# Retention of the first 768 tokens: two tokens to a partition, 64-row tiles, all masks ahead of v, decays about the middle of 256 tokens

## The chip, the cores and the metric

The kernel runs on one core of a Trainium2 chip. The metric is the device time of one execution in microseconds (us), 205.38 as the median of three runs before the change (205.08 to 205.7). Engines: PE is the tensor engine (PEld its weight loads), DVE the vector engine, ACT the scalar engine, POOL is GpSimd, SP issues most DMAs; "SPq" and "ACTq" are the queues of SP and ACT that issue DMAs.

## The reference

A retention layer (a linear attention whose state decays) for 4 batches, 8 heads, 768 tokens and 64 channels a head feeds a two-layer network with mish as its activation:

```python
gamma = 1.0 - 2.0 ** (-5.0 - np.arange(H))            # one decay per head
for t in range(S):
    state = gamma * state + einsum('bhd,bhe->bhde', k[:, :, t], v[:, :, t])
    y[:, :, t] = einsum('bhd,bhde->bhe', q[:, :, t], state) / sqrt(D)
x = y.transpose(0, 2, 1, 3).reshape(B * S, H * D)      # 3072 x 512
h = x @ w_in                                           # 512 x 2048
out = (h * tanh(log1p(exp(h)))) @ w_out                # 2048 x 512
```

## The kernel before

The retention is computed in chunks. A chunk is 128 tokens of one batch, all 8 heads (six chunks a batch, 24 in all, number `g`). Within a chunk: scores are k transposed times q (`at`, in PSUM, the matmuls' memory), a mask keeps what is not ahead of its token (`am`, by DVE), `present` multiplies `am` with v, `past` adds q times the state of the chunk before, `outer` is k times v, summed into the state. The decay is put on q, k or v as a power of gamma when the fp32 inputs are cast to fp16 (`casts`, L220), and a state is multiplied by gamma^128 when it is handed on (`gcm` L309, `gch` L451). The result is written, transposed, as `xt`.

The network takes tokens in blocks: block 0 has four chunks (512 tokens), every later one two. `g1` (L540) is the first matrix product with mish by ACT, `g2_mm` (L561) the second, `seven` (L626) the second product of the blocks from 2 on in a form with seven products in place of eight; it needs sums of w_out parts, `tmat` (L599 to L602), which DVE computes during block 1.

The order of instructions on each engine is the order in which the program issues them; nothing is moved by a scheduler. Each engine works its own queue in that order, and an instruction waits for the data and the buffers that it needs.

Block 0 (`first_block`, L725): SP loads the first q in two halves (four tokens to a partition, so 1024 contiguous bytes each), then k and v of chunk 0, 1, 2, 3 in turn (one token to a partition, 256 contiguous bytes for each head), then w_in in six loads, w_out in three, and q and v of chunk 4. Scores have 64 rows (channels of one head) and 128 columns, `present` 128 rows and 64 columns, and `outer`, `past` and the state's addition by an identity matmul use all 128 rows and columns, two heads at a time. `spin` (L250) issues matmuls whose result nobody reads; they fill PE's time while it waits. k is cast by ACT (L229), v by POOL (L233). Behind the retention DVE casts w_in (`cast_win`, L161, eight half slices) as it lands.

While block 0 runs through `g1` and `g2_mm`, `plan` (L769) hangs further work behind numbered steps: casts of w_out, the loads of chunks 4 and 5 (`load_more`, three of them issued by ACT), their casts, transposes by PE (`turn`), scores, state and `y_two` for block 1. From chunk 6 on, q and k are transposed by DMA (`turn_by_dma`, L237), and the retention runs in tiles of 64 rows and 64 columns, so that four matmuls with different quarters of the array can work at a time (`score`, `outer_half`, `y_mm`); a half chunk's state is `mid` (L436), a chunk's state is `suh` and `sth` (L445). A one-column copy of the result (`seen`, L522) stands between matmuls that add to the same PSUM bank from different rows. Buffers come from rotating pools; a pool's `bufs` is how many there are.

Of the kernel before, what the change touches and what calls it, by code (L numbers as in the profile page):

```python
# [16 lines left out]
def kernel(  # L17
# [12 lines left out]
    P = 128  # L30
# [16 lines left out]
    gamma = (1.0 - 2.0 ** (-5.0 - np.arange(H))).astype(np.float64)  # L47
    jj = np.arange(C)
    mid = (C - 1) / 2.0
    qs_np = np.stack([BOOST * scale * g ** (jj - mid) for g in gamma], 1).astype(np.float32)  # L50
    vs_np = np.stack([BOOST * g ** (mid - jj) for g in gamma], 1).astype(np.float32)
    spread = [qs_np[(jj * CPB + r) % C] for r in range(CPB)]
    boost_np = np.full((C, H), BOOST, np.float32)
    qvs_np = np.ascontiguousarray(np.concatenate([qs_np, vs_np, *spread, boost_np], 1))
# [5 lines left out]
    tpp = ctx.enter_context(tc.tile_pool(name="rn_tp", bufs=2))  # L60
# [14 lines left out]
    qvs = cpool.tile([P, (3 + CPB) * H], FP32, name="qvs")  # L75
    nc.scalar.dma_start(qvs, nc.inline_tensor(qvs_np, name="qvs_c").ap())
    qs, vs = qvs[:, :H], qvs[:, H:2 * H]
    qs_spread = qvs[:, 2 * H:(2 + CPB) * H].rearrange("p (r h) -> p h r", r=CPB)
    boosts = qvs[:, (2 + CPB) * H:]
    ident = cpool.tile([P, P], FP16, name="ident")  # L80
    tri = cpool.tile([P, C], FP32, name="tri")
    gcm = cpool.tile([P, HP, P], FP32, name="gcm")
    gch = cpool.tile([P, HP, D], FP32, name="gch")
    warm = cpool.tile([P, 1], FP32, name="warm")
# [4 lines left out]
    nc.gpsimd.memset(tri, 0.0)  # L89
    nc.gpsimd.affine_select(  # L90
        out=tri, in_=tri, compare_op=ALU.is_gt, fill=1.0, base=0,
        pattern=[[-1, C]], channel_multiplier=1)

    tri_half = cpool.tile([P, D], FP32, name="tri_half")

    tri_first = cpool.tile([P, CPB, C // CPB], FP32, name="tri_first")
    nc.gpsimd.memset(tri_first, 0.0)
    nc.gpsimd.affine_select(
        out=tri_first, in_=tri_first, compare_op=ALU.is_gt, fill=1.0, base=0,
        pattern=[[-1, CPB], [-CPB, C // CPB]], channel_multiplier=1)  # L100
# [4 lines left out]
    nc.vector.memset(gcm, 0.0)  # L105
    for h in range(H):
        o = 64 * (h % 2)
        nc.vector.memset(gcm[o:o + 64, h // 2, o:o + 64], float(gamma[h] ** C))

# [3 lines left out]
    qfirst_t = cpool.tile([P, HP, CPB, P], FP16, name="qfirst_t")  # L113
# [9 lines left out]
    def room(g):  # L123
        loaded[g] = [
            None if nm == "q" and g < CPB else
            lpool.tile([P, H, D], FP32, name=nm + "f", tag=nm + "f", bufs=4 if nm == "q" else 6)
            for nm in "qkv"]
# [67 lines left out]
    def turn_first_q(qf, half, on_act):  # L195
        a, n = half * (H // 2), H // 2
        q16 = castp.tile([P, CPB, n, D], FP16, name="qfirst16", bufs=1, tag=f"qfirst16_{half}")
        nc.vector.tensor_tensor(
            q16.rearrange("p r h d -> p h r d"), qf[:, a:a + n],
            qs_spread[:, a:a + n].unsqueeze(3).broadcast_to((P, n, CPB, D)), op=ALU.mult)  # L200
        t_ps = mmps.tile([P, n // 2, CPB, P], FP16, name="t_ps", tag="mm")
        for i in range(n // 2):
            for r in range(CPB):
                nc.tensor.transpose(t_ps[:, i, r], q16[:, r, 2 * i:2 * i + 2], ident)
        dst = qfirst_t[:, a // 2:(a + n) // 2]
        if on_act:
            nc.scalar.copy(dst, t_ps)
        else:
            nc.vector.tensor_copy(dst, t_ps)

    def turn_k(g):
        k16 = cast[g][1]
        t_ps = mmps.tile([P, HP, C], FP16, name="t_ps", tag="mm")
# [705 lines left out]
```

## Time and profile before

| what | us |
|---|---|
| median of three runs | 205.38 |
| profiled execution | 205.68 |
| its span | 203.9 |
| granted TensorE clock | 0.998 |
| first w_in matmul (L549) starts | 19.58 |
| first w_out matmul (L563) starts | 33.70 |
| block 1's first w_in matmul starts | 51.37 |
| block 2's first w_in matmul starts | 67.92 |

```profile
## 2 busy tenths in 40 slices
PE   7998999999999999999999998999999999999993
PEld 2554444445864788887888887888888888888882
DVE  3696554257999448459596564736854953655062
ACT  2333665043541452452363362463363453541640
POOL 3245000426995141952645616606607500000000
PEclk9999999999999999999999999999999999999999
DMA  5999999999999999699999999999990710200102
GB/s 178 238 220 342 379 387 365 224 304 205 206 230 250 220 223 217 145 204 247 170 171 279 195 195 258 184 200 256 171 195 3 159 50 3 103 3 35 71 27 77
```

Each column is one fortieth of the span, 5.1 us. A digit is the busy share of the engine in tenths. GB/s is what the DMA engines moved: about 220 in the second and third column, where k and v of block 0 are loaded, and 340 to 390 in the next four, where the weights are.

A line of the timeline has start, duration, engine, line, operation, tile written and read, shape, count, and in brackets the idle time ahead of it with what ended it.

### The profile page before, as it was taken

The page shows a single profiled execution, that of the slowest core. Times are in us where ns is not written, and L with a number is a line of the kernel's source. Part 1 is how long each engine was busy: PE and PEld are TensorE (multiplying, and loading weights), DVE is VectorE, ACT ScalarE, POOL GpSimd, SP SyncE. Part 2 cuts the span into 40 slices and gives each one's busy share as a digit, 9 for nine tenths or more (in the row PEclk, how much of TensorE's full clock was granted, in tenths as well). Part 3 has the DMA queues.
Part 4 walks back from the last instruction along what each step waited for, and adds up shares of the span by engine and source line. Part 5 has one row for each costly group of instructions (what it writes and reads, how often), then busy time and mean ns, then how long its engine had stood idle before and what let it go on. Part 6 is the DMA issues. An engine that isn't in the chain of part 4 may idle for free.

```text
span 203.9 us, 6059 instructions
## 1 busy us (share of the span) xinstructions
PE 196.7 (96%) x2629; PEld 149.7 (73%) x2629; DVE 121.4 (60%) x217; ACT 86.7 (43%) x154; POOL 72.3 (35%) x88
## 2 busy tenths in 40 slices
PE   7998999999999999999999998999999999999993
PEld 2554444445864788887888887888888888888882
DVE  3696554257999448459596564736854953655062
ACT  2333665043541452452363362463363453541640
POOL 3245000426995141952645616606607500000000
PEclk9999999999999999999999999999999999999999
DMA  5999999999999999699999999999990710200102
GB/s 178 238 220 342 379 387 365 224 304 205 206 230 250 220 223 217 145 204 247 170 171 279 195 195 258 184 200 256 171 195 3 159 50 3 103 3 35 71 27 77
DMA packets 99994, 38.69 MB, mean 190 GB/s; under 512 B 90496, under 2 KB 94080, under 8 KB 99968
## 3 DMA queue, kind: packets, MB, share of 16 engines
q1 hardware_dynamic: 96704, 37.50, 87.0%
q10 hardware_dynamic: 3264, 0.82, 2.4%
q8 instruction: 20, 0.33, 0.7%
q14 instruction: 6, 0.05, 0.1%
HBM read 27.29 MB, written 6.29 MB: 165 GB/s over the span
## 4 chain that ended last, share of the span: by engine, by line
PE 67%; DMA 12%; SPq 9%; DVE 8%; POOL 1%; issue 1%; ACT 1%; DVEq 0%; ACTq 0%
PE h_ps L549 33%; PE o_ps L646 23%; SPq L131 7%; DMA kf<-in_k_dram 6%; PE o_ps L563 4%; DMA wi<-in_moe_w_in_dram 3%; PE y_ps L482 3%; DMA qkt<-qk 2%; DVE tmat L601 1%; DVE tmat L602 1%; DVE tmat L599 1%; PE at L398 1%; SPq L239 1%; DVE tmat L600 1%; PE u_ps L405 1%
## 5 line engine op out<-in xcount | busy, mean ns | idle before, releaser
L549 PE MATMUL h_ps<-xt,win 128*128 128x256 f16 (+1 forms) x704 | 86.4, 282 | 0.7 <-DVE win L166 0.5
L549 PEld LDWEIGHTS <-win 128*128 128x128 f16 x704 | 68.4, 98 | 16.6 <-DVE win L166 1.0
L557 ACT ACTIVATE g<-h_ps 128x512 f16<-128x512 f32 x96 | 57.3, 597 | 49.2 <-PE h_ps L549 49.2
L233 POOL TENSOR_TENSOR v<-vf,qvs 128x512 f16<-128x512 f32 x24 | 27.5, 1146 | 19.0 <-DMA vf<-in_v_dram 18.8
L226 POOL TENSOR_TENSOR qk<-qf,qvs 128x512 f16<-128x512 f32 x20 | 20.9, 1046 | 30.3 <-DMA qf<-in_q_dram 24.1
L646 PEld LDWEIGHTS <-gsum 128*128 128x128 f16 x288 | 27.0, 98 | 3.9 <-DVE gsum L615 0.2
L646 PE MATMUL o_ps<-tmat,gsum 128*128 128x256 f16 x216 | 26.6, 273 | 0.0
L646 PEld LDWEIGHTS <-g 128*128 128x128 f16 x216 | 21.1, 98 | 2.4
L563 PE MATMUL o_ps<-wout,g 128*128 128x512 f16 x96 | 22.6, 380 | 0.0
L231 POOL TENSOR_TENSOR qk<-kf,qvs 128x512 f16<-128x512 f32 x18 | 21.1, 1171 | 1.5 <-DMA kf<-in_k_dram 1.3
L615 DVE TENSOR_TENSOR gsum<-g 128x512 f16<-128x512 f16 x18 | 9.1, 508 | 19.5 <-ACT g L557 19.4
L652 ACT COPY snap<-o_ps 128x256 f32<-128x256 f32 x27 | 10.0, 372 | 19.5 <-PE o_ps L646 19.5
L660 DVE TENSOR_TENSOR osb<-o_ps,snap 128x256 f32<-128x256 f32 x27 | 11.4, 424 | 10.8 <-PE o_ps L646 6.8
L646 PE MATMUL o_ps<-wout,g 128*128 128x256 f16 x144 | 17.2, 273 | 0.0
L563 PEld LDWEIGHTS <-g 128*128 128x128 f16 x96 | 8.8, 98 | 9.4
L822 POOL COPY summed<-gsum 128x1 f16<-128x1 f16 x6 | 1.1, 187 | 36.7 <-DVE gsum L620 26.4
L536 ACT CAST xt<-y_ps 128x512 f16<-128x512 f32 x13 | 7.2, 587 | 15.2 <-PE y_ps L482 15.2
L442 DVE TENSOR_TENSOR mid<-u_ps,sth 128x256 f16<-128x256 f32 x15 | 6.3, 422 | 11.4 <-PE u_ps L405 11.1
L253 PE MATMUL at<-ident 128*128 128x512 f16 (+1 forms) x34 | 10.3, 429 | 1.4 <-POOL ident L86 1.4
L471 DVE TENSOR_TENSOR am<-at,tri_half 128x1024 f16<-128x1024 f32 x9 | 10.9, 1214 | 0.0
L451 DVE TENSOR_TENSOR sth<-suh,gch 128x256 f16<-128x256 f32 x15 | 9.0, 602 | 0.6
L646 PE MATMUL o_ps<-wout,gsum 128*128 128x256 f16 x72 | 9.4, 273 | 0.0
(81 smaller groups left out, 176.5 us busy)
## 6 DMA issues: line engine op xcount, KB each, us to landing
kf<-in_k_dram SPq DMA_DIRECT2D x23, 256.0 KB, 5.1
vf<-in_v_dram SPq DMA_DIRECT2D x23, 256.0 KB, 5.3
out_dram<-osb SPq DMA_DIRECT2D x22, 256.0 KB, 3.2
qf<-in_q_dram SPq DMA_DIRECT2D x19, 256.0 KB, 5.2
wt<-in_moe_w_out_dram SPq DMA_DIRECT2D x3, 1024.0 KB, 10.1
wi<-in_moe_w_in_dram SPq DMA_DIRECT2D x4, 512.0 KB, 7.4
wi<-in_moe_w_in_dram SPq DMA_DIRECT2D x2, 1024.0 KB, 10.8
qfirst<-in_q_dram SPq DMA_DIRECT2D x2, 512.0 KB, 4.6
```

Of the source, the lines that this page charges most:

```text
L131: queue.dma_start(loaded[g][n], (q, k, v)[n][b, :, c * C:(c + 1) * C].rearrange("h p d -> p h d"))
L226: nc.gpsimd.tensor_tensor(q16, qf, qs.unsqueeze(2).broadcast_to((P, H, D)), op=ALU.mult)
L231: nc.gpsimd.tensor_tensor(k16, kf, boosts.unsqueeze(2).broadcast_to((P, H, D)), op=ALU.mult)
L233: nc.gpsimd.tensor_tensor(v16, vf, vs.unsqueeze(2).broadcast_to((P, H, D)), op=ALU.mult)
L253: nc.tensor.matmul(ats[g][:, 0, :m], ident, ident.unsqueeze(1).broadcast_to((P, m, P)), start=True, stop=True)
L471: nc.vector.tensor_tensor(am.rearrange("p a j i c -> p (a j i) c"), at.rearrange("p a j i c -> p (a j i) c"), tri_half.unsqueeze(1).broadc ...
L549: nc.tensor.matmul(h_ps[:, j], wins[s][f // 2][:, bp, f % 2 * P:(f % 2 + 1) * P], xts[blk][:, bp, :nt], start=(bp == 0), stop=(bp == NBP - 1))
L557: nc.scalar.activation(gt, h_ps, AF.Mish, scale=inv_boost3)
L563: nc.tensor.matmul(o_ps, gts[blk, fb][:, t * P:(t + 1) * P], wouts[s][:, f, cols], start=(fb == 0), stop=(fb == NFB - 1))
L646: nc.tensor.matmul(o_ps, x(f), w(f), start=first and f == 0, stop=f == n - 1, skip_group_check=True)
L652: nc.scalar.copy(x, o_ps)
L660: nc.vector.tensor_tensor(dst, o_ps, plus, op=ALU.add)
```

## The change

Three pairs of chunks (0 and 1, 2 and 3, 4 and 5: `n` = 0, 1, 2) are now handled as 256 tokens each. Partition p holds tokens 2p and 2p + 1, so that q (of pair 2), k and v are loaded in pieces of 512 contiguous bytes, each in two halves `a` of four heads, 256 KB a load. SP's order is first q, all k of pairs 0 and 1, all v of pairs 0 and 1, w_in, w_out, then q, k, v of pair 2. For pairs 0 and 1 POOL casts k with the decay and ACT casts v without it. Every retention matmul of the three pairs has 64 rows and 64 columns (`m` is the half of the partitions, 128 tokens each; `hh` the head of a pair of heads). All scores and masks of block 0 come ahead of its first use of v. The state of the middle of a pair is not multiplied; `gch` is gamma^256 and is applied once a pair, in later blocks too (`state_of`). The masks and `gch` are made by POOL, ahead of its casts of k and right behind them; `tri`, `tri_first`, `gcm`, `qfirst_t` and the functions for 128-row chunks are gone. The diff, without removed lines that the kernel above shows:

```diff
     gamma = (1.0 - 2.0 ** (-5.0 - np.arange(H))).astype(np.float64)
+    pos = np.arange(2 * C)
+    mid = (2 * C - 1) / 2.0
+    qs_np = np.stack([BOOST * scale * g ** (pos - mid) for g in gamma], 1).astype(np.float32)
+    vs_np = np.stack([BOOST * g ** (mid - pos) for g in gamma], 1).astype(np.float32)
     jj = np.arange(C)
-    mid = (C - 1) / 2.0
-    qs_np = np.stack([BOOST * scale * g ** (jj - mid) for g in gamma], 1).astype(np.float32)
-    vs_np = np.stack([BOOST * g ** (mid - jj) for g in gamma], 1).astype(np.float32)
-    spread = [qs_np[(jj * CPB + r) % C] for r in range(CPB)]
-    boost_np = np.full((C, H), BOOST, np.float32)
-    qvs_np = np.ascontiguousarray(np.concatenate([qs_np, vs_np, *spread, boost_np], 1))
+    tables = [qs_np[:C], qs_np[C:], vs_np[:C], vs_np[C:]]
+    tables += [qs_np[(jj * CPB + r) % (2 * C)] for r in range(CPB)]
+    tables += [qs_np[2 * jj + r] for r in range(2)]
+    tables += [vs_np[2 * jj + r] for r in range(2)]
+    tables += [np.full((C, H), BOOST, np.float32)]
+    qvs_np = np.ascontiguousarray(np.concatenate(tables, 1))
...
-    tpp = ctx.enter_context(tc.tile_pool(name="rn_tp", bufs=2))
+    tpp = ctx.enter_context(tc.tile_pool(name="rn_tp", bufs=4))
...
+    def keep_from(t, rows, pattern):
+        nc.gpsimd.memset(t, 0.0)
+        for n in range(2):
+            nc.gpsimd.affine_select(
+                out=t[n * D:(n + 1) * D], in_=t[n * D:(n + 1) * D], compare_op=ALU.is_gt,
+                fill=1.0, base=0, pattern=pattern, channel_multiplier=rows)
+
+    keep_from(keep_four, 2, [[1, 2], [-1, CPB], [-CPB, C // CPB]])
+    for h in range(H):
+        nc.gpsimd.memset(
+            gch[64 * (h % 2):64 * (h % 2) + 64, h // 2], float(gamma[h] ** (2 * C)))
...
+    def turn_parts(parts, dst, on_act=False):
+        t_ps = mmps.tile(list(dst.shape), FP16, name="t_ps", tag="mm")
+        turn_into(parts, dst, t_ps, on_act)
+
+    def turn_into(parts, dst, t_ps, on_act):
+        for i in range(dst.shape[1]):
+            for r in range(dst.shape[2]):
+                nc.tensor.transpose(t_ps[:, i, r], parts(i, r), ident)
...
+    def load_pair(n, nm, a, queue):
+        src = {"q": q, "k": k, "v": v}[nm]
+        queue.dma_start(
+            pairs[n][nm][a],
+            src[0, a * (H // 2):(a + 1) * (H // 2), n * 2 * C:(n + 1) * 2 * C].rearrange(
+                "h (p r) d -> p h r d", r=2))
+
+    def cast_pair(n, nm, a, scales=None, on=None):
+        src = pairs[n][nm][a]
+        if nm == "v":
+            t = castp.tile([P, 2, H // 2, D], FP16, name="v16", bufs=7)
+        else:
+            if a == 0:
+                pairs[n, nm] = castp.tile([P, 2, 2, H // 2, D], FP16, name="qk16", bufs=4)
+            t = pairs[n, nm][:, a]
+        pairs[n, nm, a] = t
+        dst = t.rearrange("p r h d -> p h r d")
+        if scales is None:
+            nc.scalar.mul(dst, src, BOOST)
+        else:
+            (on or nc.gpsimd).tensor_tensor(
+                dst, src, scales[:, a * (H // 2):(a + 1) * (H // 2)].unsqueeze(3).broadcast_to(
+                    (P, H // 2, 2, D)), op=ALU.mult)
+
+    def turn_pair(n, nm, a, on_act):
+        if a == 0:
+            pairs[n, nm + "t"] = qktp.tile([P, HP, 2, C], FP16, name="qkt", bufs=6)
+        t = pairs[n, nm, a]
+        turn_parts(lambda i, r: t[:, r, 2 * i:2 * i + 2],
+                   pairs[n, nm + "t"][:, a * (HP // 2):(a + 1) * (HP // 2)], on_act)
...
+    def pair_scores(n, a):
+        if (n, "at", a) not in pairs:
+            pair_at(n, a)
+        at, kt = pairs.pop((n, "at", a)), pairs[n, "kt"]
+        for i in range(HP // 2):
+            for r in range(2):
+                for m in range(2):
+                    for hh in range(2):
+                        b = a * (HP // 2) + i
+                        nc.tensor.matmul(
+                            as_q(at[half(m), hh, i, r], n), kt[half(hh), b, r, half(m)],
+                            pair_q(n, b, hh, m), start=True, stop=True)
+        am = tpp.tile([P, 2, HP // 2, 2, C], FP16, name="am")
+        keep = keep_four if n < 2 else keep_two
+        nc.vector.tensor_tensor(
+            am.rearrange("p h i r c -> p (h i) (r c)"),
+            at.rearrange("p h i r c -> p (h i) (r c)"),
+            keep.rearrange("p s r c -> p (s r c)").unsqueeze(1).broadcast_to((P, HP, 2 * C)),
+            op=ALU.mult)
+        pairs[n, "am", a] = am
...
+    def pair_outer(n, u, a):
+        k16, v16 = pairs[n, "k", a], pairs[n, "v", a]
+        for r in range(2):
+            for i in range(HP // 2):
+                for m in range(len(u)):
+                    for hh in range(2):
+                        nc.tensor.matmul(
+                            u[m][half(hh), a * (HP // 2) + i],
+                            k16[half(m), r, 2 * i + hh], v16[half(m), r, 2 * i + hh],
+                            start=a == 0 and r == 0 and i == 0, stop=True,
+                            skip_group_check=True)
+
+    def pair_state(n, u, m):
+        g = 2 * n + m
+        if m == 0:
+            st = stp.tile([P, HP, D], FP16, name="mid")
+            if n == 0:
+                nc.vector.tensor_copy(st, u[0])
+            else:
+                nc.vector.tensor_tensor(st, u[0], states[g - 1], op=ALU.add)
+        else:
+            su = stp.tile([P, HP, D], FP32, name="suh")
+            nc.vector.tensor_tensor(su, u[1], states[g - 1], op=ALU.add)
+            st = stp.tile([P, HP, D], FP16, name="sth")
+            nc.vector.tensor_tensor(st, su, gch, op=ALU.mult)
+        states[g] = st
+
+    def pair_present(n, y, a):
+        am, v16 = pairs[n, "am", a], pairs[n, "v", a]
+        for i in range(HP // 2):
+            for r in range(2):
+                for m in range(2):
+                    for hh in range(2):
+                        nc.tensor.matmul(
+                            y[m][half(hh), a * (HP // 2) + i], v16[half(m), r, 2 * i + hh],
+                            am[half(m), hh, i, r], start=a == 0 and i == 0 and r == 0,
+                            stop=True, skip_group_check=True)
+
+    def pair_past(n, y, m):
+        st = states[2 * n + m - 1]
         for i in range(HP):
-            nc.tensor.transpose(t_ps[:, i], k16[:, 2 * i:2 * i + 2], ident)
-        kt = qktp.tile([P, HP, C], FP16, name="kt", bufs=2)
-        nc.vector.tensor_copy(kt, t_ps)
-        qkts[g] = (qfirst_t[:, :, :, g * (C // CPB):(g + 1) * (C // CPB)], kt)
+            for hh in range(2):
+                nc.tensor.matmul(
+                    as_q(y[m][half(hh), i], n), st[half(hh), i], pair_q(n, i, hh, m),
+                    start=False, stop=True, skip_group_check=True)
...
+    def pair_xt(n, y, m, on_act=True):
+        blk = n // 2
+        if blk not in xts:
+            xts[blk] = xtp.tile([P, HP, TB], FP16, name="xt")
+        if blk == 0:
+            dst = xt_first(2 * n + m)
+        else:
+            dst = xts[blk][:, :, :2 * C].rearrange(
+                "p i (r c) -> p i r c", r=2)[:, :, :, half(m)]
+        src = y[m].rearrange("p i (r c) -> p i r c", r=dst.shape[2])
+        if on_act:
+            nc.scalar.copy(dst, src)
+        else:
+            nc.vector.tensor_copy(dst, src)
...
     def state_of(g):
         u = us.pop(g)
-        if not last_of_batch(g):
+        if last_of_batch(g):
+            return
+        st = stp.tile([P, HP, D], FP16, name="sth")
+        if g % 2 == 0:
+            nc.vector.tensor_tensor(st, u[:, 1], mids[g], op=ALU.add)
+        else:
             su = stp.tile([P, HP, D], FP32, name="suh")
             nc.vector.tensor_tensor(su, u[:, 1], mids[g], op=ALU.add)
-            st = stp.tile([P, HP, D], FP16, name="sth")
             nc.vector.tensor_tensor(st, su, gch, op=ALU.mult)
-            states[g] = st
+        states[g] = st
 
...
+        room_pair(2, "qkv")
+        for nm in "qkv":
+            for a in range(2):
+                load_pair(2, nm, a, nc.sync)
 
     def load_more():
-        load_one(CPB, 1, nc.scalar)
-        load_one(CPB + 1, 0, nc.scalar)
-        load_one(CPB + 1, 2, nc.scalar)
-        load_one(CPB + 1, 1, nc.sync)
         load_last_wout(0)
         load_last_wout(1)
-        nload[0] += 2
+        nload[0] = ncast[0] = CPB + 2
         load_to(CPB + 4)
 
     def first_block():
-        for g in range(CPB):
-            room(g)
         qf = load_first_q()
-        for g in range(CPB):
-            load_one(g, 1, nc.sync)
-            load_one(g, 2, nc.sync)
-        nload[0] = CPB
+        for n in range(2):
+            room_pair(n)
+        for nm in "kv":
+            for n in range(2):
+                for a in range(2):
+                    load_pair(n, nm, a, nc.sync)
         load_weights()
...
+        pair_at(0, 0)
+        spin(50)
         turn_first_q(qf, 0, True)
...
+        spin(14)
         turn_first_q(qf, 1, False)
...
         for n in range(2):
...
+            for a in range(2):
+                cast_pair(n, "k", a, vs_two)
+        nc.gpsimd.memset(tri_half, 0.0)
+        for n in range(2):
+            nc.gpsimd.affine_select(
+                out=tri_half[half(n)], in_=tri_half[half(n)], compare_op=ALU.is_gt, fill=1.0,
+                base=0, pattern=[[-1, D]], channel_multiplier=1)
+        keep_from(keep_two, 2, [[1, 2], [-1, 2], [-2, D]])
+        turn_pair(0, "k", 0, True)
+        spin(6)
+        pair_scores(0, 0)
+        pair_at(0, 1)
+        spin(2)
+        turn_pair(0, "k", 1, True)
+        spin(6)
+        pair_scores(0, 1)
+        pair_at(1, 0)
+        spin(2)
+        turn_pair(1, "k", 0, True)
+        spin(4)
+        cast_pair(0, "v", 0)
+        pair_scores(1, 0)
+        pair_at(1, 1)
+        spin(2)
+        turn_pair(1, "k", 1, True)
+        for n, a in ((0, 1), (1, 0), (1, 1)):
+            cast_pair(n, "v", a)
+        spin(4)
+        pair_scores(1, 1)
+        u = [mmps.tile([P, HP, D], FP32, name="u_ps", tag="mm") for _ in range(2)]
+        for a in range(2):
+            pair_outer(0, u, a)
+        for m in range(2):
+            pair_state(0, u, m)
+        y = [pool.tile([P, HP, C], FP32, name="y_ps", tag=tag)
+             for pool, tag in ((mmps, "mm"), (pxps, "px"))]
+        for a in range(2):
+            pair_present(0, y, a)
+        pair_xt(0, y, 0)
+        nc.scalar.copy(seen, y[1][:, 0, :1])
+        pair_past(0, y, 1)
+        pair_xt(0, y, 1)
+        u = banks("u_ps", D)
+        for a in range(2):
+            pair_outer(1, u, a)
+        pair_state(1, u, 0)
+        y = banks("y_ps", C)
+        for a in range(2):
+            pair_present(1, y, a)
+        for m in range(2):
+            nc.scalar.copy(seen, y[m][:, 0, :1])
+        pair_past(1, y, 0)
+        pair_past(1, y, 1)
+        pair_xt(1, y, 0, False)
+        pair_xt(1, y, 1)
         cast_win(0)
...
+        pair_state(1, u, 1)
         for s in range(1, NSL):
             cast_win(s)
+
+        def cast_qk():
+            for a in range(2):
+                cast_pair(2, "q", a, qs_two)
+            for a in range(2):
+                cast_pair(2, "k", a)
+            for a in range(2):
+                cast_pair(2, "v", a, vs_two)
+
+        def turn_two():
+            t_ps = atps.tile([P, 2, HP, 2, C], FP16, name="t_ps", tag="at")
+            for j, nm in enumerate("qk"):
+                pairs[2, nm + "t"] = qktp.tile([P, HP, 2, C], FP16, name="qkt", bufs=6)
+                turn_into(
+                    lambda i, r: pairs[2, nm, i // 2][:, r, i % 2 * 2:i % 2 * 2 + 2],
+                    pairs[2, nm + "t"], t_ps[:, j], nm == "k")
+
         plan = {
             9: [(cast_wout, 0)],
             12: [(cast_wout, 1)],
...
+            16: [(cast_wout, 2), (load_more,), (cast_qk,)],
+            23: [(cast_wout, 3, True)],
+            25: [(turn_two,)],
+            26: [(pair_scores, 2, 0)],
+            27: [(pair_scores, 2, 1)],
+            28: [(next_chunk, CPB + 2), (next_chunk, CPB + 3)],
+            29: [(outer_two,)],
+            31: [(y_two,)],
         }
...
+    def banks(name, width):
+        t = atps.tile([P, 2, TB], FP32, name=name, tag="at")
+        return [t[:, m, :HP * width].rearrange("p (i c) -> p i c", i=HP) for m in range(2)]
+
+    def outer_two():
+        u = banks("u_ps", D)[:1]
+        for a in range(2):
+            pair_outer(2, u, a)
+        pair_state(2, u, 0)
+
+    def y_two():
+        y = banks("y_ps", C)
+        for a in range(2):
+            pair_present(2, y, a)
+        for m in range(2):
+            nc.scalar.copy(seen, y[m][:, 0, :1])
+        for m in range(2):
+            pair_past(2, y, m)
+        for m in range(2):
+            pair_xt(2, y, m)
```

`banks` gives two PSUM banks of one `at` buffer. `pair_q` gives the transposed q of a pair, `as_q` views a result in the token order of q, `pair_at` takes an `at` buffer, `keep_four` and `keep_two` are the masks for q with four and with two tokens to a partition.

## The prediction

> **What bounds the kernel now.** I read the busy shares first, then the waits of TensorE, then the chain of waits, then the timeline of the first 20 us and of 50 to 68 us.
>
> ```profile
> PE 196.7 (96%) x2629; PEld 149.7 (73%) x2629; DVE 121.4 (60%) x217; ACT 86.7 (43%) x154; POOL 72.3 (35%) x88
> PE at L398 <- DMA qkt<-qk: 0.6, 1, 0.6
> PE h_ps L549 <- DVE win L166: 0.5, 1, 0.5
> PE t_ps L263 <- ACT qk L229: 0.3, 1, 0.3
> PE y_ps L482 <- DVE sth L451: 0.3, 1, 0.3
> ```
>
> PE is 96% busy, and its waits after the start are short. So a change can win only in two places: the 19.6 us before the first h_ps matmul, where much of PE's busy time is spin matmuls, and these few waits.
>
> ```profile
> 12.12 1.14 SPq L149
> 13.31 6.94 DMA wi<-in_moe_w_in_dram
> 20.27 0.69 DVE win L166
> ```
>
> In the chain of waits the first 20 us belong to SP's queue and to loads. The timeline shows the rate:
>
> ```profile
> 8.92 1.04 POOL L233 TENSOR_TENSOR v<-vf,qvs 128x512 f16<-128x512 f32 x1 [6.57 <-DMA vf<-in_v_dram]
> 11.26 1.04 POOL L233 TENSOR_TENSOR v<-vf,qvs 128x512 f16<-128x512 f32 x1 [1.29 <-DMA vf<-in_v_dram]
> 13.66 1.04 POOL L233 TENSOR_TENSOR v<-vf,qvs 128x512 f16<-128x512 f32 x1 [1.37 <-DMA vf<-in_v_dram]
> 16.01 1.04 POOL L233 TENSOR_TENSOR v<-vf,qvs 128x512 f16<-128x512 f32 x1 [1.30 <-DMA vf<-in_v_dram]
> 17.60 0.58 ACT L351 CAST xt<-y_ps 128x512 f16<-128x512 f32 x1 [1.67 <-PE y_ps L325]
> 18.77 0.75 DVE L166 CAST win<-wi 128x1024 f16<-128x1024 f32 x1 [0.54 <-DMA wi<-in_moe_w_in_dram]
> 19.58 0.61 PE L549 MATMUL h_ps<-xt,win 128*128 128x512 f16 x2 [0.45 <-DVE win L166]
> ```
>
> One chunk's k and v (512 KB) land every 2.36 us, so 1.18 us per 256 KB. The 1024-byte pieces of the first q ran at 385 GB/s (windows 3.0 to 5.0 us), the 256-byte pieces of k and v at 218 (windows 6.5 to 15). The retention ends at about 19.0 (L360) and the first w_in half is cast at 19.52: both paths end together.
>
> **The change, part by part.** The base is the profiled run: span 203.9, time 205.68, which is 0.30 above the median of the runs, 205.38. I add the differences to the median.
>
> *Loads.* A 512-byte piece is in no row. Bounds: 1.18 us per 256 KB (no gain) and 0.68 us (385 GB/s). Per piece and engine the rows give 18.4 ns at 256 bytes (1.18 us, 64 pieces) and 42.6 ns at 1024 (385 GB/s over 16 engines); on a line between them 512 bytes cost 26.5 ns, or 0.85 us. I take 0.8. The first q is usable at 6.40 as before, the first k quarter (half the heads of 256 tokens) at about 7.3, the last v at 6.40 + 8 x 0.8 + 0.2 = 13.0 instead of 16.0. The page "DMA: Bandwidth & Descriptors" of the Trainium skill (Specifications) puts line rate at 512 bytes and up; by it the quarter would be usable 0.1 us sooner and the sum 0.1 us lower.
>
> *Masks ahead of v.* Each quarter goes POOL cast, transposes, ACT copy, scores, mask. POOL: 1.04 us (L233 above), first from 7.3 to 8.35; gch and the first mask table (10 memsets and 2 selects, 0.15 to 0.4 us each by L762 and L98) are done by 4.5. Then PE transposes 0.40 (four, as L215), ACT copies 128x512: 0.59 by the line through L207 (1.01 at 1024) and L652 (0.37 at 256). First scores at 9.45, first mask at 9.9. The next transposes stand behind these scores in PE's queue, so a quarter takes copy 0.59, hand-over 0.06, scores 0.25, change back to 128 rows and spin 0.25, transposes 0.44: 1.6 us, more than POOL's 1.13 and DVE's 1.22 (L285). Fourth scores at 14.25. ACT gets there at 14.2 with three v casts to go: 0.63 each (L229), 0.54 in a row: 15.8.
>
> *Tail of the first block.* Now a relay of PE and ACT: xt 0.58 to 16.35, seen 0.2 to 16.5 (warm L104: 0.20), past 0.4, xt 0.58 to 17.55, meanwhile outer and present of the second pair to 17.65, two seen reads to 18.0, past to 18.45, xt on DVE 0.69 (L534) to 19.2, and only behind it in DVE's queue the cast of w_in, 0.69. First h_ps at 19.95, 0.37 later than now. The w_in halves (2.6 to 3 us earlier) are then all there, and the waits between 19.58 and 33.70 go: 14.12 less 64 x 0.2157 is 0.32. Net +0.05. The state's DVE steps (0.42, 0.42, 0.48 after the last mask at 15.9) lie beside ACT's relay; cover gone, they cost what they exceed it by.
>
> *Tokens 512 to 767, inside 33.7 to 51.4.* Removed: 0.43 between the q and k transposes (waiting for L229), since all six loads now go ahead of the last w_out on SP's queue and land about 8 us sooner; ACT's three issues (0.4 to 3.9 us) go too. Added: scores in 64-row form, 0.52 a block against 0.39 (42.39 to 42.78), +0.26; the k copy on ACT (1.01 against 0.69, behind one step of 0.86), +0.1; the 64-row outer between 128-row matmuls, each change of form costing (PEld idles 0.42 before 64-row blocks at 61.03 and 66.64): +0.2; y: present 0.45, past 0.45, change 0.3, wait for seen 0.35 (0 to 0.65: the four matmuls behind it stand in line), 1.55 against 1.14, +0.4. Sum: 0.26 + 0.1 + 0.2 + 0.4 - 0.43 = +0.53.
>
> *Later blocks.* An even chunk's state loses its multiply:
>
> ```profile
> 63.46 0.41 DVE L440 CAST mid<-u_ps 128x256 f16<-128x256 f32 x1
> 63.90 0.42 DVE L449 TENSOR_TENSOR suh<-u_ps,mid 128x256 f32<-128x256 f32 x1
> 64.43 0.48 DVE L451 TENSOR_TENSOR sth<-suh,gch 128x256 f16<-128x256 f32 x1
> 64.40 0.31 PE L482 MATMUL y_ps<-qkt,mid 64*64 64x64 f16 x8
> 64.97 0.31 PE L482 MATMUL y_ps<-qkt,sth 64*64 64x64 f16 x8 [0.26 <-DVE sth L451]
> 65.42 0.31 PE L482 MATMUL y_ps<-qkt,mid 64*64 64x64 f16 x8
> ```
>
> Eight such matmuls take 0.14 where nothing holds them (79.28 to 79.42), here 0.57 and 0.45: 0.74 lost to the DVE chain. That chain is late because the eight tmat subtractions take 11.5 us; beside POOL they take 1.53, alone 0.94 (59.69). With loads sooner by 2.6 to 5 us, POOL's casts of chunks 6 and 7 fall before that stretch, and 0.51 goes with L451. I take -0.9: 0.74, and 0.16 of the wait for the mask and the seen read (66.42) behind it. Bounds 0 and -1.0. What is late next is nothing there: PE's own matmuls.
>
> *The wait at 125.7* (0.62, transposed q and k). The 256-byte pieces saturate the queues again from 95 us on, but POOL's casts from 80 us on are tied to DVE's sums, thus to PE, so much of the lead is used up. Bounds 0 and -0.62; I take half, -0.3.
>
> Sum: +0.05 + 0.53 - 0.9 - 0.3 = -0.62, so 205.06 for a run like the profiled one, and 204.76, in short 204.8, against the median.
>
> **Rivals.** (1) *The relay is longer than I count.* The first gemm changes its bound from a load to some 20 hand-overs of PE, ACT and DVE; 0.07 more on each puts it at 21.35. For it: PE's queue stands at each copy and each seen, and nothing is issued past them. Against: hand-overs now take 0.05 to 0.1 (L229 ends 8.38, transposes 8.44). From a start at 20.57 on (0.62 after 19.95) it eats the whole gain; at 21.35 the sum is 1.40 - 0.62 = +0.78, so 206.2. (2) *PE's clock falls.* Without spins after the fourth scores PE works under half of the time from 14.5 to 20. In the first 5 us here the 512-column spin matmuls came every 0.43 us, and then every 0.21. If that returned for 3.8 us of h_ps, it costs 1.9: 206.7. Against: the granted clock is 1.00 in every window now, and my longest gap is 1.5 us. The page "TensorE: Matmul & The Clock Gate" of the Trainium skill (Part 1) has the clock drop after an idle window of about 3.4 us; by that it stays up. (3) *512-byte pieces land no faster*, so the change doesn't do what it says: last v at 16.1, ACT's cast to 16.75, the relay after it 1.0 later, 20.95: +1.05 for the first block; the later terms stay, -0.67 in all, less some 0.4 for the smaller lead: 205.38 + 1.05 - 0.27 = 206.2. (4) *The relay is shorter* (quarters at 1.4 instead of 1.6, and the whole 0.62 at 125.7 goes): -0.62 - 0.6 - 0.3 = -1.5, so 203.9. It speaks for it that the ACT copies may overlap (0.09 in a row now).
>
> **How the numbers follow.** Forecast 0.40, its own range 204.1 to 205.4; relay longer 0.22; clock 0.06; loads no faster 0.06; relay shorter 0.26. A measurement of this kernel can tell 0.3% (0.6 us) from no change: faster means under 204.76, slower over 206.0. The forecast lies on the first bound: 0.21 faster, 0.19 same. The longer relay is 0.18 slower and 0.04 same, the clock's fall slower, loads no faster half and half, the shorter relay 0.25 faster and 0.01 same. Faster 0.21 + 0.25 = 0.46, same 0.19 + 0.04 + 0.03 + 0.01 = 0.27, slower 0.18 + 0.06 + 0.03 = 0.27. The range reaches from beyond the shorter relay to beyond the longer one, 203.4 to 206.5; outside it lie the clock's case and the far parts of the others.
>
> **What would show it.** Right: last v cast or its landing near 13; scores about 1.6 us apart; first h_ps within 19.5 to 20.4 and no wait for win behind it; tmat near 1.0 to 1.3 us, mid, sth, mid without PE gaps. Wrong: h_ps after 20.57, granted clock under 1.00, k casts 1.18 apart on POOL, or PE waiting for ACT's seen over 0.65.

## The result, and the profile after

| what | before | after |
|---|---|---|
| median of four runs each, same chip | 205.54 (205.08 to 206.84) | 211.38 (211.28 to 212.96) |
| profiled execution | 205.68 | 211.39 |
| its span | 203.9 | 209.6 |
| granted TensorE clock | 0.998 | 0.984 |
| first w_in matmul starts | 19.58 | 23.01 |
| first w_out matmul starts | 33.70 | 38.79 |
| block 1's first w_in matmul starts | 51.37 | 58.30 |
| block 2's first w_in matmul starts | 67.92 | 74.08 |

The changed kernel is slower: the ratio is 1.029, 95% interval 1.022 to 1.036. The 5.7 us of span come stage by stage: 3.43 up to the first w_in matmul, 1.66 in block 0's first product (15.78 against 14.12), 1.84 from there to block 1's (19.51 against 17.67), then 0.77 are won in block 1 (15.78 against 16.55) and 0.46 behind it.

Lines of the page of the kernel after: busy shares, granted clock by slice, and the queue that brings instructions (packets, MB, share).

```profile
span 209.6 us, 6381 instructions
...
PE 196.3 (94%) x2794; PEld 149.8 (71%) x2794; DVE 108.2 (52%) x195; ACT 89.7 (43%) x163; POOL 72.5 (35%) x91
...
PEclk9999599999999999999999999999999999999999
...
q8 instruction: 22, 0.36, 0.7%
```

One digit of the clock differs from before: the fifth slice, 21 to 26 us, has the clock at half. PE's list of waits has new entries, among them these:

```profile
PE u_ps L300 <- issue: 2.4, 1, 2.4
...
PE t_ps L205 <- DVE qkt L209: 0.8, 1, 0.8
PE y_ps L336 <- ACT seen L877: 0.5, 1, 0.5
```

"issue" says that PE waited for nothing that the profile shows: no tile, no buffer, no DMA of the program. The timeline of the first block shows where:

```profile
16.48 0.35 PEld L300 LDWEIGHTS <-qk 64*64 64x64 f16 x26
...
16.53 0.41 PE L300 MATMUL u_ps<-v,qk 64*64 64x64 f16 x23
...
19.31 0.22 PE L300 MATMUL u_ps<-v,qk 64*64 64x64 f16 x3 [2.36 <-issue]
...
21.65 0.69 DVE L353 CAST xt<-y_ps 128x512 f16<-128x512 f32 x1 [1.66 <-PE y_ps L336]
...
22.37 0.59 ACT L351 CAST xt<-y_ps 128x512 f16<-128x512 f32 x1 [1.94 <-DVE xt L353]
...
23.01 1.45 PE L560 MATMUL h_ps<-xt,win 128*128 128x512 f16 x3 [1.47 <-ACT xt L351]
```

PE stops inside one `outer`, with three of its 32 matmuls left and all their operands there, and goes on 2.36 us later. The windows (length, busy time and count of each engine, clock, DMA share, GB/s) give the clock:

```profile
15.00:20.00 5.00, 1.81 (x111) 1.42 (x99) 2.51 (x5) 1.84 (x5) 0.00 (x0) 1.00 1.09 359
20.00:25.00 5.00, 3.05 (x21) 1.55 (x21) 3.32 (x7) 0.98 (x4) 0.00 (x0) 0.52 0.99 332
25.00:30.00 5.00, 5.00 (x20) 2.09 (x19) 3.73 (x6) 2.82 (x5) 0.00 (x0) 0.80 0.95 315
```

PE is busy for 1.81 of the 5 us from 15 to 20, and then works at half its clock from 20.19 to 27.02. The two losses of the first 39 us are these. The one of 1.84 lies in `turn_two` and `y_two`:

```profile
47.95 0.61 PE L205 MATMUL t_ps<-ident,qk 128*128 128x128 f16 x8 [0.78 <-DVE qkt L209]
49.66 0.42 PE L282 MATMUL at<-qkt 64*64 64x128 f16 x16 [0.24 <-ACT qkt L207]
...
56.51 0.41 PE L336 MATMUL y_ps<-qkt,sth 64*64 64x128 f16 x8 [0.51 <-ACT seen L877]
```

And the lines that answer to the `mid` and `sth` matmuls of before:

```profile
71.33 0.31 PE L493 MATMUL y_ps<-qkt,mid 64*64 64x64 f16 x8
71.48 0.29 PE L493 MATMUL y_ps<-qkt,sth 64*64 64x64 f16 x8
71.60 0.29 PE L493 MATMUL y_ps<-qkt,mid 64*64 64x64 f16 x8
```

They started 0.57 and 0.45 apart; now it is 0.15 and 0.12. This gain came as foreseen.

**What "issue" hides.** The queue "instruction" brings 22 packets, 0.36 MB: 16 KB each. PE's two times 2794 instructions over 22 are 254, so a packet holds about 256, or 128 pairs of a weight load and a matmul. From the start of PE's matmuls and of these packets in the trace:

```
              matmul at     PE starts    packet for the     PE starts    from packet's  idle of
kernel        the border    behind it    next border        its first    end to it      PE there
before        98            14.03        16.40 to 17.49     33.05        15.56          none
after         98            12.81        16.59 to 17.68     19.31         1.63          2.36
```

Numbers of matmuls here and in the expectations are places in PE's stream, counted in pairs; the trace's own count is 3 lower in the kernel after, so its 224th matmul ends the idle time. In the experiments the trace's 352nd and 2016th matmul end such a stop, one and fourteen times 128 later: so place 227 is the first of a piece, and the border before it is at 98, 226 less 128. In these rows the packet comes some microseconds after PE has crossed a border, and it brings what stands behind the next border. Before, PE then spends 15 us more on the piece in hand. After, 64-row tiles have twice the instructions for the same work: 16 + 32 + 32 + 8 + 29 = 117 pairs went between 14.21 and 16.94, and PE had reached matmul 226 before the packet had landed. That is theory A of the expectations below: PE ran out of instructions, and the clock fell because PE was idle.

### The profile page after: what moved, and what is told of

The parts are those of the page before. It is cut to its first block, busy times and chain, and to the rows that moved or that the text cites. A ratio compares the mean times of both kernels' runs of the same rounds, so it can differ in the third digit from the quotient of the medians.

```text
span 209.6 us, 6381 instructions
## 1 busy us (share of the span) xinstructions
PE 196.3 (94%) x2794; PEld 149.8 (71%) x2794; DVE 108.2 (52%) x195; ACT 89.7 (43%) x163; POOL 72.5 (35%) x91
## 4 chain that ended last, share of the span: by engine, by line
PE 88%; ACT 4%; DMA 3%; issue 2%; DVE 1%; POOL 1%; SPq 0%; POOLq 0%; ACTq 0%; DVEq 0%
PE h_ps L560 41%; PE o_ps L660 27%; PE o_ps L574 9%; PE y_ps L493 4%; DMA kf<-in_k_dram 3%; ACT qkt L207 2%; PE at L405 1%; PE u_ps L412 1%; PE t_ps L205 1%; ACT xt L351 1%; PE y_ps L336 1%; PE at L282 1%; ACT v L248 1%; POOL qk L250 1%; PE y_ps L327 1%
## 5 line engine op out<-in xcount | busy, mean ns | idle before, releaser
L560 PE MATMUL h_ps<-xt,win 128*128 128x256 f16 (+1 forms) x704 | 88.3, 286 | 1.9 <-ACT xt L351 1.7
L364 POOL TENSOR_TENSOR v<-vf,qvs 128x512 f16<-128x512 f32 x18 | 20.6, 1145 | 1.6 <-DMA vf<-in_v_dram 1.5
L629 DVE TENSOR_TENSOR gsum<-g 128x512 f16<-128x512 f16 x18 | 7.9, 439 | 25.6 <-ACT g L568 25.6
L362 POOL TENSOR_TENSOR qk<-kf,qvs 128x512 f16<-128x512 f32 x18 | 20.3, 1125 | 0.2
L383 PE MATMUL at<-ident 128*128 128x512 f16 (+1 forms) x26 | 8.9, 470 | 1.4 <-POOL ident L96 1.4
```

Source lines behind the costliest of these rows:

```text
L362: nc.gpsimd.tensor_tensor(k16, kf, boosts.unsqueeze(2).broadcast_to((P, H, D)), op=ALU.mult)
L364: nc.gpsimd.tensor_tensor(v16, vf, vs[g % 2].unsqueeze(2).broadcast_to((P, H, D)), op=ALU.mult)
L383: nc.tensor.matmul(to[:, 0, :m], ident, ident.unsqueeze(1).broadcast_to((P, m, P)), start=True, stop=True)
L560: nc.tensor.matmul(h_ps[:, j], wins[s][f // 2][:, bp, f % 2 * P:(f % 2 + 1) * P], xts[blk][:, bp, :nt], start=(bp == 0), stop=(bp == NBP - 1))
```

## The experiments

Each time is the median of its runs, with the kernel before on the same chip beside it.

**Move the border: e1_early67.** The 13 spin matmuls of 512 columns ahead of the first q become 80 small ones that take as long; 67 more pairs lie ahead of the retention.

```diff
-        spin(50)
+        small = pairs[0, "at", 0].rearrange("p h i r c -> p h (i r) c")
+        for _ in range(80):
+            nc.tensor.matmul(
+                small[:D, 0, 0, :80], ident[:, :D], ident[:, :80], start=True, stop=True)
```

> The 13 spin matmuls of spin(50) become 80 small ones (64 rows of weights, 80 columns) in about the same 5.4 us, so PE's stream has 67 more pairs of load and matmul ahead of the retention. Theory A (PE's instructions come in 16 KB pieces of 256, two pieces ahead at most, and a piece asked for at about 13.1 was there only at 19.3): the borders move 67 pairs forward in the work, the first piece is asked for near 8.5 and is there before 15; the 2.36 us idle of PE at 16.9 is gone, the granted clock stays 1.00, first h_ps at 20.0 to 20.6 instead of 23.0, and the time is 206.2 to 207.2 instead of 211.4. Theory B (the idle belongs to a buffer or a semaphore of u_ps): the idle stays between the same two matmuls, time 211.4. Theory C (the clock falls anyway, from PE's low use after the last spin, without the long idle): first h_ps near 20.5, granted clock still near 0.5 in the five us after, time 208.5 to 209.

206.76 (206.03 to 207.89) against 205.37; ratio 1.0073 (1.0039 to 1.0106). The packet came at 10.17 to 11.36, and matmul 227 started at 14.93 with no idle time:

```profile
16.57 0.44 PE L300 MATMUL u_ps<-v,qk 64*64 64x64 f16 x26
16.82 0.65 PE L327 MATMUL y_ps<-am,v 64*64 64x128 f16 x32
...
20.07 1.24 PE L560 MATMUL h_ps<-xt,win 128*128 128x512 f16 x5 [1.47 <-ACT xt L351]
```

The first w_in matmul starts 2.94 earlier and block 0's first product takes 13.81. More instructions, and 4.6 of the 6.0 us are back.

**A smaller shift: e2_early30.** The same with 43 wider small matmuls, so 30 more pairs.

> 43 small matmuls (128 columns) in place of the 13, so 30 pairs more ahead of the retention. Theory A: PE stands idle exactly 30 pairs earlier in the work than in the changed kernel (there after 226 matmuls in all, which is the 38th of the second pair's... of the last third of the first block; here after 226 in all again, now in the last matmuls of present or in past of the first pair), and for about 0.5 to 1.5 us instead of 2.4, since the piece is asked for some 2 us earlier. Clock 1.00 or a short fall. 206.5 to 209. Theory B: idle at the same matmul of outer, 2.4 us, 211.4.

212.81 in one run. The stall was expected 30 pairs earlier and did not come: the packet had ended at 14.81, and matmul 227 started at 16.45. The borders of all later pieces had moved too, and one fell where half chunks lie densely:

```profile
PE y_ps L493 <- issue: 1.9, 1, 1.9
...
PE at L405 <- DMA qkt<-qk: 1.4, 1, 1.4
```

The first, 1.88, stands behind matmul 2018 = 98 + 15 x 128. And the clock fell although PE's longest gap between 14 and 20 us, from one start to the next, was 1.72:

```profile
15.00:20.00 5.00, 2.28 (x131) 1.92 (x115) 3.84 (x8) 2.77 (x8) 0.00 (x0) 1.00 1.09 358
20.00:25.00 5.00, 4.95 (x16) 1.94 (x17) 3.84 (x7) 1.67 (x4) 0.00 (x0) 0.66 1.05 388
```

So the first half of theory A stands and the second needs mending: it is low use, not one long stop, that lets the clock fall. The traces say how low. The granted clock changes only at steps of 3.41 us, which start at another time in each run, and it follows PE's busy share in the step just ended:

```
kernel         step of 3.41 us      PE busy       clock in the step behind it
after           16.78 to  20.19     0.83  (24%)   0.50
e2_early30      17.10 to  20.51     1.45  (42%)   0.50
e6_split        17.07 to  20.48     1.44  (42%)   0.50
e5_dve         124.18 to 127.59     1.50  (44%)   0.50
e2_early30     143.39 to 146.81     1.60  (47%)   0.50
e1_early67      15.87 to  19.28     1.76  (52%)   1.00
b1_before63    126.03 to 129.44     1.89  (55%)   1.00
e8_border       16.98 to  20.39     2.85  (83%)   1.00
```

In all twelve traces, once the clock is up, each step with at most 47% is followed by half the clock and each with 52% or more by the full one. e1_early67 is as little busy as e2_early30 from 15 to 20 us (2.30 of 5) and kept its clock because its steps happened to lie otherwise: that was luck.

**The same in the kernel before: b1_before63.** Its first spins become 77 small matmuls, 63 more pairs; nothing else is changed.

```diff
-        spin(0, 54)
+        small = ats[0]
+        for _ in range(77):
+            nc.tensor.matmul(
+                small[:D, 0, 0, :80], ident[:, :D], ident[:, :80], start=True, stop=True)
```

> The kernel before the change, its 14 first spin matmuls replaced by 77 small ones (63 pairs more) in about the same time; nothing else. Theory A: the borders of 16 KB pieces lie at PE matmul 226 + 128 n in every kernel; with 63 more pairs the border 1890 comes to stand one matmul ahead of the end of a dense stretch of 64-row matmuls (retain of a later block, near 140 us), where the idle of 1.9 us stood with 30 more pairs in the changed kernel (there border 2018, near 145 us). So a wait without releaser of 1 to 2.5 us appears after matmul 1890, the first block stays as it was (first h_ps 19.3 to 19.8), and the time is 206.5 to 209. Theory B (the idle of the changed kernel is one of its own waits): no such idle, 204.3 to 206.7.

209.21 in one run, against 205.66. The list of PE's waits has

```profile
PE at L398 <- DMA qkt<-qk: 1.5, 1, 1.5
...
PE o_ps L646 <- issue: 1.2, 1, 1.2
```

and the second stands exactly at the border at 1890. It ends at the trace's 1887th matmul; two semaphore instructions of PE that the kernel after has not (12.51 and 15.78 in this trace) fill one place more. The border costs 1.20 of the 3.55. The first block, expected unchanged, starts its first product at 20.15, 0.57 late, behind a wait of 0.97 for a mask at 12.67. The trace of the kernel before has no such stop: it was quick in part because no border of it fell into a dense stretch. Four of the stalls seen, with two borders that were passed just in time (e3_turn, below, stops for 2.56 where the kernel after does):

```
                    PE starts    packet for the      first matmul    from packet's
kernel              behind       border after        of that piece   end to it
after, stall        98:  12.81   16.59 to 17.68       227:  19.31    1.63
e7_tail, stall      226: 14.86   18.84 to 19.97       355:  21.46    1.49
e2_early30, stall   1890: 143.51 144.08 to 145.36    2019: 146.88    1.52
b1_before63, stall  1762: 142.19 142.46 to 143.67    1891: 145.19    1.52
e2_early30, none    98:  11.19   13.67 to 14.81       227:  16.45    1.64
e9_best, none       226: 14.95   18.80 to 19.92       355:  21.97    2.05
```

In the two stalls while inputs load, the piece came into use 6.5 to 6.6 us after the border before it was crossed, in the two later ones 3.0 to 3.4. The Trainium skill, page "Runtime: NRT & Kernel Launch" (Instruction fetch mechanics), has the sequencer fetch blocks of 16 KB, 256 instructions, while it executes the block before; the packets here agree. It also calls the cost of a border mostly hidden; by this case it is hidden as long as 128 pairs take PE longer than that, and costs up to 2.6 us where they don't.

**The loss in block 1's retention: e3_turn, e4_both.** `turn_two` gets a PSUM tile for q and one for k; e4_both has the 80 small matmuls as well.

```diff
-            t_ps = atps.tile([P, 2, HP, 2, C], FP16, name="t_ps", tag="at")
-            for j, nm in enumerate("qk"):
+            for nm in "qk":
+                t_ps = atps.tile([P, HP, 2, C], FP16, name="t_ps", tag="at")
...
-                    pairs[2, nm + "t"], t_ps[:, j], nm == "k")
+                    pairs[2, nm + "t"], t_ps, nm == "k")
```

> turn_two takes one PSUM buffer for q and another for k, so that the transposes of k need not wait until DVE has copied q out of the shared one. If that wait (0.78 us on PE at 47.9, and the ACT copy of k that comes later for it) is what I did not count: the stretch from the first w_out matmul to block 1's first w_in matmul, 19.35 us in the changed kernel, becomes 18.2 to 18.7, and the time 210.3 to 210.8. If the wait is another's: no difference, 211.4.

> Both edits. If they are independent, 211.4 less what each gave: 205.2 to 206.3, so level with the kernel before (205.4). If the gain of the second is eaten by a later wait: the same time as with the small spins alone.

e3_turn: 210.4 in one run; the transposes of k follow those of q at once, and the stage is 18.57, 0.94 less. e4_both: 206.72 (206.01 to 207.85), no better than e1_early67; its stage is 19.40 (33.86 to 53.26). With PE on time, something else ends last:

```profile
42.60 1.05 ACT L177 CAST wout<-wt 128x1024 f16<-128x1024 f32 x1 [0.41 <-DMA wt<-in_moe_w_out_dram]
43.56 1.01 ACT L207 COPY qkt<-t_ps 128x1024 f16<-128x1024 f16 x1
44.62 0.42 PE L282 MATMUL at<-qkt 64*64 64x128 f16 x16 [1.07 <-ACT qkt L207]
```

The copy of k stands in ACT's queue behind a cast of w_out, and that one waits for its load. In e3_turn, where PE comes here 5 us later, that cast ended at 46.16, 1.66 ahead of the copy.

**Both copies on DVE: e5_dve.** e4_both with `t_ps, False` in place of `nm == "k"`.

> Early small spins, separate PSUM buffers for q and k in turn_two, and k copied out by DVE instead of ACT, which with early spins copies w_out's last slice until 43.6. If the queue of ACT is what took back the gain of separate buffers: first w_out matmul to block 1's first w_in matmul 18.4 to 18.8 us (19.5 with the spins alone, 19.4 with separate buffers), time near 205.7 to 206.2. If DVE is held too: 19.2 or more.

The stage is 18.40, as expected (20.09, 33.90 and 52.30 are the three starts):

```profile
42.31 1.29 DVE L209 COPY qkt<-t_ps 128x1024 f16<-128x1024 f16 x2 [6.57 <-PE t_ps L205]
...
43.66 0.42 PE L282 MATMUL at<-qkt 64*64 64x128 f16 x16
```

The one run took 208.65 all the same. At 125.2 PE waited 1.91 for a transposed q or k, and the clock stood at half from 127.59 to 131.00, right behind the step with that wait (the 44% of the table above). This wait was 0.62 before, nothing in the kernel after and in e3_turn, and 0.37 to 1.92 in the others of this study, without a relation to the edits that I can see; it is a spread of some 1.5 us that medians only partly take out.

**The wait for seen: e6_split.** e5_dve, with `present` and the two reads of `seen` one planned step ahead of `past`.

```diff
             29: [(outer_two,)],
+            30: [(present_two,)],
             31: [(y_two,)],
```

> As before, and present of tokens 512 to 767 goes one step (four w_out matmuls, 0.86 us) ahead of past, so that the seen copies lie beside those matmuls. If PE's wait for seen (0.51) and one change of form are what is left there: 17.9 to 18.3 us for the stretch, 205.2 to 205.9 in all. A change of form more (0.45) may eat it: then 18.4 to 18.8.

The wait of 0.51 is gone, the stage is 17.94 (before 17.67). 205.79 (204.92 to 206.83) against 205.66; ratio 1.0002 (0.9970 to 1.0034). Its ten runs fall in two groups: six at a clock of 0.998 to 1.000, 204.92 to 205.95, and four at 0.990 to 0.992, 206.33 to 206.83.

**PE kept busy ahead of the first product: e7_tail.** e6_split with six matmuls that nobody reads, behind the last `past`.

```diff
         pair_past(1, y, 1)
+        idle = mmps.tile([P, HP, C], FP32, name="h_ps", tag="mm")
+        for _ in range(6):
+            nc.tensor.matmul(
+                idle, ident, ident.unsqueeze(1).broadcast_to((P, HP, P)), start=True, stop=True)
         pair_xt(1, y, 0, False)
```

> As before, with six 512-column spin matmuls in the 1.5 us in which PE waits for the last xt of block 0. If the clock is on the edge there (with early spins alone it was 0.990 to 1.000 over the runs, and the runs at 0.99 took 207.5 to 207.9): every run at 0.997 or more, the spread of the runs smaller, the median 0.2 to 0.5 lower than without. First h_ps no later than 20.1. If the spread has another cause: same spread, same median.

All ten runs had a clock of 0.997 or more, 205.26 to 206.11; the median stayed at 205.79. The windows:

```profile
15.00:20.00 5.00, 3.66 (x133) 2.40 (x119) 3.84 (x8) 2.74 (x8) 0.00 (x0) 1.00 1.09 356
20.00:25.00 5.00, 4.57 (x21) 2.06 (x22) 3.81 (x7) 2.39 (x4) 0.00 (x0) 1.00 1.05 387
```

Of the 0.43 missing from 20 to 25, 0.41 is a new stop behind matmul 354 = 226 + 128: the six pairs moved the next border ahead of its packet (in the table of stalls above), and block 0's first product took 14.38.

**The border back, and a shorter tail: e8_border, e9_best.** e8_border has 74 small matmuls of 87 columns ahead, so that as many pairs lie ahead of the first product as in e6_split. e9_best also lets ACT make both copies of the last xt.

```diff
-        for _ in range(80):
+        for _ in range(74):
...
-        pair_xt(1, y, 0, False)
+        pair_xt(1, y, 0)
```

> As e7_tail, but with 74 small matmuls ahead of the first q in place of 80, each 87 columns wide in place of 80, so in the same time; with the six matmuls in the wait for the last xt the first block then has as many pairs as in e6_split. Theory A (PE's instructions come in pieces of 128 pairs, and a border that falls into a dense stretch while the next piece is still on its way costs): the gap of 0.79 us behind matmul 354 goes, the h_ps stage is 13.8 instead of 14.38, the piece is asked for as in e6_split; 205.2 at the median, from 205.79. Rival (the six matmuls themselves, their PSUM tile or the reads behind it cost the 0.57): the stage stays at 14.3 to 14.4 and the time at 205.8.

> e8_border with both halves of the first block's last xt copied by ACT, so that DVE casts w_in as soon as it lands. If the hand-over DVE to ACT (1.5 us between PE's last past and the second xt) sets the first h_ps, the first h_ps starts at 19.8 instead of 20.03 and the time is 0.2 lower than that of e8_border, some 205.0, below the kernel before (205.4) by less than 0.3 per cent. Rival (ACT's two copies in a row take as long as DVE's and ACT's did): first h_ps at 20.0 or later, no change.

e8_border: the stop is gone, the product takes 13.81; 205.38 (204.48 to 208.8) against 205.34, ratio 0.9993 (0.9963 to 1.0023). e9_best: 204.57 (204.15 to 206.79), ratio 0.9972 (0.9943 to 1.0000).

```profile
17.74 1.29 DVE L169 CAST win<-wi 128x1024 f16<-128x1024 f32 x2
...
18.61 1.07 ACT L351 CAST xt<-y_ps 128x512 f16<-128x512 f32 x2 [0.72 <-PE y_ps L336]
...
19.81 1.89 PE L560 MATMUL h_ps<-xt,win 128*128 128x512 f16 x8
```

The start at 19.81 is the one expected; the time fell by 0.8, not 0.2, and 1.44 of the difference between the two profiled executions (1.9) is the wait near 125 (1.92 in the one, 0.48 in the other). With e7_tail, 32 of 34 runs with the six matmuls had the clock at 0.997 or more; of the 30 of e1_early67, e4_both and e6_split, which have the small matmuls ahead and not the six, 22. Where the clock fell in the runs without a trace is not known; of the 19 runs of the kernel before beside e6_split two were at 0.989 as well. e9_best beats the changed kernel by about 3%; over the kernel before its gain of 0.3% is likely, but the interval reaches to no change.

## Why the prediction was wrong, step by step

**Right.** The bound: the first 20 us and a few waits are all there was to win. The first scores at 9.61 (forecast 9.45), a quarter every 1.53 (1.6), the fourth scores at 14.21 (14.25), the v casts done at 15.72 (15.8), the first xt at 15.62 as the relay has it. The relay itself: with instructions at hand, e1_early67 starts the first product at 20.07 (19.95), and it takes 13.81 (13.80). So rival (1), the relay longer by its hand-overs, is refuted: what was late was one stop, not twenty hand-overs. One of the signs of being wrong, a wait for seen over 0.65, did show (0.81 at 16.31), but e1_early67 has it too (0.81 at 16.35) and starts in time. Block 1's state chain gave 0.77 in the kernel after and 0.74 to 0.78 in e5_dve to e9_best (0.9, bounds 0 and 1.0).

**Mis-sized.** The loads: I took 0.8 us per 256 KB in 512-byte pieces; 291 GB/s from 6.5 to 11.5 are 0.90. This decided nothing, since POOL's casts followed each other without a wait. By the page "DMA: Bandwidth & Descriptors" of the Trainium skill (Specifications) such pieces reach line rate; the trace has 291 GB/s beside 385 for 1024 bytes, so here they don't.

**The first step that failed** is "Tail of the first block", where outer and present of the second pair end at 17.65, as if PE could issue whatever has its operands. It could not: 2.36 of the 3.43 is the stop at 16.94, 0.58 what is left behind it, which I put down to the slow clock from 20.19 on, and 0.49 the relay (20.07 less 19.58), of which 0.37 were forecast. No rival names such a stop. I named each queue of SP, ACT and POOL, and not the one that feeds PE itself, though the page of before has it (20 packets), and from the fourth scores to the last `present` the program has 16 + 32 + 32 + 8 + 32 + 32 = 152 pairs, which take 3.3 us in e1_early67 (14.2 to 17.5), where the kernel before issues 61 matmuls in the 5 us up to 19.5.

**The second** is the chance of rival (2), the clock: 0.06, because "my longest gap is 1.5 us". The price was right: 1.9 forecast, and 1.97 measured in the product (15.78 less 13.81), with 0.58 more ahead of it (2.94 less 2.36). The argument was wrong: e2_early30 has no gap over 1.72 and the clock fell, in e6_split it fell too (in four of ten runs the mean clock is 0.990 to 0.992), and filling the last gap held it up in e8_border, whose steps lie like theirs. Not the longest gap counts but the busy share of a step. The page "TensorE: Matmul & The Clock Gate" of the Trainium skill (Part 1) has the clock drop after an idle window of some 3.4 us, with windows that run freely. The steps of 3.41 us with a start of their own in each run agree; that a window must be idle throughout does not agree with e2_early30, which was busy for 42% of it.

**The third** is the sum for tokens 512 to 767: +0.53, measured +1.84. The term of -0.43 for the wait between the transposes of q and k became +0.35: the load is early as forecast, but q and k now share one PSUM tile, and PE waits with k's part until DVE has copied q's (0.78). A tile for each and k's copy on DVE together were worth 1.11 (19.51 to 18.40). The wait for seen was sized at 0.35 with a bound of 0.65, and measures 0.51; taking it out gave 0.46. What is left over before is 0.27 (17.94 against 17.67), with the old wait of 0.43 gone: so by this difference the 64-row forms together, with one change of form more in e6_split, cost 0.70, where I had 0.26 + 0.2 and, in y, 0.05.

**The fourth**, -0.3 for the wait at 125.7, looks right in the kernel after, where the wait of 0.62 is gone, but that may be luck: PE comes there some 6 us late, and in the versions that come on time the wait is there in some size. Why it varies was not tried.

## What to carry to other kernels

Count the instructions that PE must issue between two points, not only their time: a stretch of small tiles that uses up 128 matmuls in a few microseconds can outrun the fetch of the next piece, and "issue" as the releaser in the middle of a loop is its mark. The place of the border depends on everything ahead of it, so an edit at the start can cost or win 2 us at its end; shift the border with dummy matmuls of the same total time before judging the edit. Judge the risk to the clock by PE's busy share in any 3.4 us (here it fell at 47% and less and held at 52% and more), not by the longest gap.

## What the runs showed of the hardware that was not expected

- PE's instructions come by DMA in pieces of 16 KB, or 128 pairs, and the stops stand where a piece begins; the matmul that ends a stop starts 1.5 to 1.6 us after the piece's packet has ended. The packet came 3.8 to 4.0 us after the border before in the stops while the inputs of block 0 load, and 0.3 to 0.6 in the two later ones; that the other traffic delays it is likely, but no run varied it.
- In e2_early30 the clock fell without any gap over 1.72 us. It is set in steps of 3.41 us, whose start differs from run to run: half for a step when PE was busy for 24 to 47% of the one before, full from 52% on. So two runs with the same low use, 2.28 and 2.30 of 5 us, went on at half and at full clock.
- Six matmuls that compute nothing cost 0.57 us some 2 us later, through the border alone; e8_border, with the same six and six fewer ahead, has not that loss.
